# Attention over a cached context for one token: values accumulated as 64 columns x 8 positions, and a reordered end

## The chip, the cores and the metric

The kernel runs on one core of a Trainium2 chip. Its engines work side by side, each on its own queue of instructions: TensorE (PE in the profile, with its weight loads as PEld), VectorE (DVE), ScalarE (ACT), GpSimd (POOL) and SyncE (SP, which here only issues DMAs). Sixteen DMA engines move data from HBM into SBUF. The metric is the device time in microseconds of one execution.

## The reference

The inputs are one token `x` of 640 values, a condition `c` of 640, caches of keys and values for 32 heads with 8192 positions of 192 values each, and weights. All numbers are 32-bit floats.

```python
mod = (_silu(c) @ w_mod).reshape(c.shape[0], 6, 1, -1)
sa, ca, ga, sb, cb, gb = (mod[:, 0], mod[:, 1], mod[:, 2], mod[:, 3], mod[:, 4], mod[:, 5])
h = _layernorm(x, axis=-1) * (1 + ca) + sa
x = x + ga * _A_ref(h, A_k_cache, A_v_cache, A_wq, A_wo)
h = _layernorm(x, axis=-1) * (1 + cb) + sb
x = x + gb * _B_ref(h, B_w1, B_b1, B_w2, B_b2)
```

`_A_ref` makes a query per head (`h @ wq`), scores all 8192 keys, takes a softmax, sums the values with its weights and multiplies the 32 x 192 results by `wo`. `_B_ref` is a two-layer network: `relu(h @ w1 + b1)` squared, times `w2`, plus `b2`; its hidden size is 1536. Keys and values are 201 MB each, the bulk of what is read.

## The kernel before

The program is fully unrolled and its order on every engine is the order in which it is written; the framework only adds the waits.

**Storage.** Everything large goes through one pool of three slots (`slot`, tag "slot") of 128 partitions, some 57 KB each. The loads are all issued by SP, in one queue, in this order: modulation weights with the first query weights (`wm0_t`), keys 0, values 0, keys 1, values 1, and so on; each takes the slot that was used three loads earlier, so that a value load waits for the keys of the head before to be worked off, and a key load for the values of the head before. A key load of the heads between also carries 1920 columns of weights (a pair's `wq` or `wo`). After keys 31 comes the first part of `wm1_t` (the last `wo` and one modulation block), after values 31 its second part (two modulation blocks), then `w1_t`, then `gw_t`: the sixth modulation block (the gate) and the twelve blocks of `w2`, in the three pieces of `W2_CUT`.

**A head.** Each partition holds 64 consecutive positions. `keys` (L177) works in four chunks of 16 positions: VectorE multiplies by the query (L184), GpSimd folds six positions in half (L187), VectorE sums nine positions (L188) and the six halves (L189), ScalarE sums one (L192). Between chunks, `between` puts in small work: `project` of the pair before (after chunk 1 of an even head), `attend` (after chunk 2 of an even head), the next `query` (after chunk 2 of an odd head); `inverse` of the head before comes after chunk 0. `softmax` (L206) takes the maximum across partitions through TensorE, and ScalarE's exponential (L216) writes each of the 64 weights 16 times, because a multiplication on a 32-column strip of TensorE wants 32 stationary columns: here two positions, 16 copies each.

**Values.** `values` (L220) makes 32 multiplications of 384 columns per head, two positions of 192 values each. The four column strips g = j % 4 take turns, and each strip accumulates its eight multiplications in 32 partitions of one PSUM bank. Rows 0 to 15 of a strip hold the sums for the first position's weights, rows 16 to 31 those for the second's; in the first half of the columns only the first are wanted, in the second half only the second. `project` (L232) picks them: two VectorE operations per head (L238, L239) with `ri`, the inverse of the softmax's sum times a two-column mask (L204). Three multiplications per pair (L242) by ones then sum over the partitions and turn the 384 results of the pair into columns; `attend` copies these (L246) and multiplies by `wo` into `att` (L250).

**The end.** After values 31: `project` and `attend` of the last pair, the residual `x1` (L297), the layernorm (L94), with the multiplications of modulation blocks 3 and 4 (`mod(3, 2, ...)`, L130) inside `scale_b`, that is, after the layernorm's second total; transposition, the first layer (L311), bias, square (L314 to L316), transposition, the gate's modulation (`mod(5, 1, ...)`), the second layer (L327) block by block, `y` (L330) and the output.

```python
        for j in range(n):
            g = j % G
            nc.tensor.matmul(ps_t[h][32 * g:32 * (g + 1), :PW], p[:, 2 * j:2 * j + 2].rearrange("p e r -> p (e r)"),
                             t[:, PW * j:PW * (j + 1)], start=(j < G), stop=(j >= n - G))
```

Of the kernel before, what the change touches and what calls it, by code (L numbers as in the profile page):

```python
# [22 lines left out]
KB = DG // 32  # L23
FB = FG // 32
PW = 2 * DH
NPAIR = H // 2
NPOS = SK // P
I = 16
# [5 lines left out]
WQ = KB * PW  # L34
HD = NPOS * DH
SLOT = HD + WO
W2_CUT = ((0, 6), (6, 5), (11, 1))
EPS = 1e-5


@with_exitstack
def block_kernel(ctx: ExitStack, tc: tile.TileContext, xc, k0, kx, k31, vc, wm0, wm1, w1, gw2, bb, out):
# [7 lines left out]
    def slot(name):  # L50
        return strm.tile([P, SLOT], F32, tag="slot", name=name, bufs=3)
# [4 lines left out]
    ones = const.tile([P, P], F32, name="ones")  # L56
    nc.vector.memset(ones, 1.0)

    mask = const.tile([P, 2], F32, name="mask")
    nc.vector.memset(mask[:, 0:1], 0.0)  # L60
    nc.vector.memset(mask[:, 1:2], 1.0)
    for g in range(G):
        nc.vector.memset(mask[32 * g:32 * g + 16, 0:1], 1.0)
        nc.vector.memset(mask[32 * g:32 * g + 16, 1:2], 0.0)
    eps_t = const.tile([P, 1], F32, name="eps_t")
    nc.vector.memset(eps_t, EPS)

# [26 lines left out]
    def layernorm(x, copies, scale1, shift, name):  # L94
# [26 lines left out]

    mods = const.tile([P, 6, DG], F32, name="mods")

    def mod(first, n, w):

        ps = psum.tile([P, 512], F32, tag="q", name=f"ps_mod{first}", bufs=2)
        for b in range(KB):
            wb = w[:, b].rearrange("p (m n) -> p m n", m=n)
            for g in range(G):
                nc.tensor.matmul(ps[32 * g:32 * (g + 1), :n * DG], e[:, b:b + 1].to_broadcast([P, 32]),  # L130
                                 wb[:, :, DG * g:DG * (g + 1)], start=(b == 0), stop=(b == KB - 1))
# [7 lines left out]
    def load(src, to, h, what):  # L139
        to[h] = slot(f"{what}{h}")  # L140
        n, w = CUTS.get((what, h), 1), src.shape[1]
        for c in range(n):
            a, b = c * HD // n, (c + 1) * HD // n if c + 1 < n else w
            nc.sync.dma_start(to[h][:, a:b], src[:, a:b])
# [3 lines left out]
        load(k0 if h == 0 else k31 if h == H - 1 else kx[h - 1], k_t, h, "k")  # L148

    def load_v(h):  # L150
        load(vc[h].rearrange("(p i) d -> p (i d)", p=P), v_t, h, "v")

    load_k(0)
    mod(0, 2, wm0_t[:, :KB * 2 * D].rearrange("p (b n) -> p b n", b=KB))
# [43 lines left out]
    ri_t, ps_t, sum_t = {}, {}, {}  # L198

    def inverse(h):  # L200
        r = work.tile([P, 1], F32, tag="r", name=f"r{h}")
        nc.vector.reciprocal(r, sum_t.pop(h))
        ri_t[h] = work.tile([P, 2], F32, tag="ri", name=f"ri{h}", bufs=3)
        nc.vector.tensor_scalar(ri_t[h], mask, r, None, op0=ALU.mult)  # L204

    def softmax(h, sc):  # L206
        mp = work.tile([P, 1], F32, tag="mp", name=f"mp{h}")
        nc.vector.tensor_reduce(mp, sc, axis=AX.X, op=ALU.max)  # L208
        ps = psum.tile([P, 512], F32, tag="sm", name=f"ps_mx{h}", bufs=2)
        nc.tensor.matmul(ps[:, :P], mp.to_broadcast([P, P]), ident, start=True, stop=True)  # L210
        nm = work.tile([P, 1], F32, tag="nm", name=f"nm{h}")
        nc.vector.tensor_reduce(nm, ps[:, :P], axis=AX.X, op=ALU.max, negate=True)  # L212

        p = work.tile([P, NPOS, 16], F32, tag="p", name=f"p{h}", bufs=1)
        sp = work.tile([P, 1], F32, tag="sp", name=f"sp{h}")
        nc.scalar.activation(p, sc[:, :, None].to_broadcast([P, NPOS, 16]), AF.Exp, bias=nm, accum_out=sp)  # L216
        sum_t[h] = total(sp, f"sum{h}")
        return p

    def values(h, p):  # L220

        t = v_t.pop(h)
        ps_t[h] = psum.tile([P, 512], F32, tag="o", name=f"ps_o{h}", bufs=3)
        n = NPOS // 2
        for j in range(n):
            g = j % G
            nc.tensor.matmul(ps_t[h][32 * g:32 * (g + 1), :PW], p[:, 2 * j:2 * j + 2].rearrange("p e r -> p (e r)"),  # L227
                             t[:, PW * j:PW * (j + 1)], start=(j < G), stop=(j >= n - G))

    os_t = {}  # L230

    def project(i):  # L232

        os_ = work.tile([P, PW], F32, tag="os", name=f"os{i}")
        for a in range(2):
            h = 2 * i + a
            o, ps, ri = os_[:, DH * a:DH * (a + 1)], ps_t.pop(h), ri_t.pop(h)
            nc.vector.tensor_scalar(o, ps[:, :DH], ri[:, 0:1], None, op0=ALU.mult)  # L238
            nc.vector.scalar_tensor_tensor(o, ps[:, DH:PW], ri[:, 1:2], o, op0=ALU.mult, op1=ALU.add)  # L239
# [16 lines left out]
    for h in range(H):  # L256
        i = h // 2
        if h:
            load_k(h)
        if h == H - 1:  # L260
            wm1_t = slot("wm1_t")
            nc.sync.dma_start(wm1_t[:, :WO + KB * D], wm1[:, :WO + KB * D])
# [12 lines left out]
        p = softmax(h, sc)  # L275
        if h == H - 1:
            mod(2, 1, wm1_t[:, WO:WO + KB * D].rearrange("p (b n) -> p b n", b=KB))
# [5 lines left out]
    nc.sync.dma_start(w1_t[:, :KB * FF], w1)  # L283
    gw_t = slot("gw_t")
    a = 0
    for b0, n in W2_CUT:
        b = KB * D + (b0 + n) * D
        nc.sync.dma_start(gw_t[:, a:b], gw2[:, a:b])
        a = b
    w1_t = w1_t[:, :KB * FF].rearrange("p (b n) -> p b n", b=KB)  # L290
    w2_t = gw_t[:, KB * D:(KB + FB) * D].rearrange("p (b n) -> p b n", b=FB)
# [25 lines left out]
    fT = columns(f, FG, "fT", work, tag="os")  # L317
# [59 lines left out]
```

## Time and profile before

| | |
|---|---|
| median of three runs | 1059.56 us (1059.51 to 1061.22) |
| profiled execution, its time | 1059.44 us |
| profiled execution, its span | 1057.7 us |
| TensorE, matmuls | 39% busy |
| VectorE | 78% |
| ScalarE | 10% |
| GpSimd | 17% |
| read from HBM | 451.82 MB, 427 GB/s over the span |
| granted TensorE clock, mean | 0.65 |

The profile is that of one execution. Its page gives the busy time of each engine, the span in 40 slices, the DMA queues, the chain of work that ended last, and the costliest groups of instructions: line, engine, operation, output<-input, shapes, count, then busy time, mean nanoseconds of one, and the idle time before them with what ended it. A landing is counted from the issue of the DMA to the arrival of its semaphore. The granted clock is a share of full speed. A multiplication of 32-bit floats stands in the trace as two matmuls and two weight loads.

### The profile page before, as it was taken

How to read it: one execution, taken by the hardware profiler on the slowest of the kernel's cores; microseconds unless marked ns; L12 is line 12 of the kernel's file. 1: busy time of each engine (PE TensorE's matmuls, PEld its weight loads, DVE VectorE, ACT ScalarE, POOL GpSimd, SP SyncE). 2: the span in 40 equal slices, each digit the busy share in tenths (PEclk: the TensorE clock that was granted, in tenths of full speed). 3: DMA queues.
4: the chain of work that ended last, by engine and by line, in shares of the span. 5: the costliest groups of instructions: out<-in, count | busy, mean ns of one | idle time of the engine just before them, and what ended most of it. 6: DMA issues, size and time to landing. Idle time of an engine off the chain costs nothing.

```text
span 1057.7 us, 7915 instructions
## 1 busy us (share of the span) xinstructions
PE 415.7 (39%) x3120; PEld 187.8 (18%) x3120; DVE 821.5 (78%) x646; ACT 110.1 (10%) x343; POOL 180.4 (17%) x134
## 2 busy tenths in 40 slices
PE   2143532435343344533344353233533334453436
PEld 1011211112121111211112121111211111121223
DVE  1976878978787986878888787897868798789962
ACT  1010011000111010110101001100011101011110
POOL 0211112211121211211212111221111221112110
PEclk9666565666656666665666666566665666666668
DMA  9999999999999999999999999999999999999997
GB/s 400 444 430 423 439 428 428 444 427 428 436 426 429 441 426 434 427 436 426 434 438 419 440 426 445 426 436 421 438 424 439 433 432 430 423 435 430 418 431 318
DMA packets 11565, 452.33 MB, mean 428 GB/s; under 512 B 1540, under 2 KB 1544, under 8 KB 1672
## 3 DMA queue, kind: packets, MB, share of 16 engines
q1 hardware_dynamic: 11240, 451.81, 99.2%
q8 instruction: 24, 0.39, 0.1%
q14 instruction: 13, 0.11, 0.0%
q10 hardware_dynamic: 288, 0.01, 0.0%
HBM read 451.82 MB, written 0.00 MB: 427 GB/s over the span
## 4 chain that ended last, share of the span: by engine, by line
DMA 43%; DVE 40%; PE 14%; ACT 2%; issue 1%; DVEq 0%; SPq 0%; ACTq 0%
DMA k<-in_kx 40%; DVE k L184 21%; DVE sc L188 13%; PE ps_o L227 10%; DVE sc L189 4%; DMA gw_t<-in_gw 2%; ACT p L216 2%; PE ps_mx L210 1%; DMA xct<-in_xc 1%; PE ps_sum L91 1%; PE ps_mod L130 1%; PE ps_q L170 1%; DVE nm L212 0%; DVE mp L208 0%; DVE ri L204 0%
## 5 line engine op out<-in xcount | busy, mean ns | idle before, releaser
L184 DVE TENSOR_TENSOR k<-k,qb 128x3072 f32<-128x3072 f32 x128 | 429.0, 3352 | 145.7 <-DMA k<-in_kx 145.7
L187 POOL TENSOR_TENSOR k<-k 128x576 f32<-128x576 f32 x128 | 179.7, 1404 | 836.0 <-DVE k L184 799.3
L188 DVE TENSOR_REDUCE sc<-k 128x9 f32<-128x1728 f32 x128 | 250.2, 1954 | 4.4
L227 PE MATMUL ps_o<-v,p 128*32 128x384 f32 x2048 | 239.3, 637 | 0.0
L210 PE MATMUL ps_mx<-ident,mp 128*128 128x128 f32 x64 | 25.4, 501 | 338.6 <-DVE mp L208 338.6
L192 ACT ACTIVATE jk<-k 128x192 f32<-128x192 f32 x128 | 46.5, 363 | 768.1 <-DVE k L184 750.0
L227 PEld LDWEIGHTS ps_o<-v,p 128*32 128x32 f32 x2048 | 75.7, 140 | 142.2 <-issue 141.6
L189 DVE TENSOR_REDUCE sc<-k 128x6 f32<-128x576 f32 x128 | 95.1, 743 | 0.1
L242 PE MATMUL ps_oT<-ones,os 128*128 128x32 f32 x96 | 26.3, 398 | 143.1 <-DVE os L239 141.1
L210 PEld LDWEIGHTS ps_mx<-ident,mp 128*128 128x128 f32 x64 | 16.0, 311 | 357.5 <-DVE mp L208 332.2
L250 PE MATMUL att<-k,oT 128*32 128x160 f32 x360 | 27.4, 474 | 75.2 <-DVE oT L246 75.2
L170 PE MATMUL ps_q<-k,hR 128*128 128x384 f32 x150 | 52.4, 497 | 0.0
L242 PEld LDWEIGHTS ps_oT<-ones,os 128*128 128x128 f32 x96 | 22.1, 308 | 156.2 <-DVE os L239 155.6
L216 ACT ACTIVATE p<-sc,nm 128x1024 f32<-128x1024 f32 x32 | 36.7, 1147 | 114.2 <-DVE nm L212 114.2
L91 PE MATMUL ps_sum<-sp,ones 128*128 128x1 f32 x64 | 18.8, 363 | 56.2 <-ACT p L216 56.2
L170 PEld LDWEIGHTS ps_q<-k,hR 128*128 128x128 f32 x150 | 27.3, 190 | 25.2 <-issue 9.4
L212 DVE TENSOR_REDUCE nm<-ps_mx 128x1 f32<-128x128 f32 x32 | 9.3, 291 | 28.5 <-PE ps_mx L210 28.5
L250 PEld LDWEIGHTS att<-k,oT 128*32 128x32 f32 x360 | 14.8, 165 | 81.4 <-DVE oT L246 77.2
L91 PEld LDWEIGHTS ps_sum<-sp,ones 128*128 128x128 f32 x64 | 16.1, 313 | 65.6 <-ACT p L216 65.6
L192 ACT ACTIVATION_READ_ACCUMULATOR jk<-k 128x1 f32 x128 | 23.9, 187 | 0.0
L130 PE MATMUL ps_mod<-wm_t,silu 128*32 128x320 f32 (+1 forms) x120 | 12.8, 608 | 14.7 <-DVE silu L120 14.7
L238 DVE TENSOR_SCALAR os<-ps_o,ri 128x192 f32<-128x192 f32 x32 | 13.1, 408 | 3.9 <-PE ps_o L227 3.9
(74 smaller groups left out, 104.4 us busy)
## 6 DMA issues: line engine op xcount, KB each, us to landing
k<-in_kx SPq DMA_DIRECT2D x29, 7104.0 KB, 26.8
v<-in_vc SPq DMA_DIRECT2D x31, 6144.0 KB, 20.7
k<-in_k SPq DMA_DIRECT2D x1, 6144.0 KB, 27.0
k<-in_k SPq DMA_DIRECT2D x4, 1536.0 KB, 19.6
v<-in_vc SPq DMA_DIRECT2D x4, 1536.0 KB, 14.8
wm_t<-in_wm SPq DMA_DIRECT2D x1, 4160.0 KB, 12.9
k<-in_kx SPq DMA_DIRECT2D x1, 4032.0 KB
w_t<-in_w SPq DMA_DIRECT2D x1, 3840.0 KB, 21.9
```

Source lines behind the costliest of these rows:

```text
L91: nc.tensor.matmul(ps[:, :1], ones, src, start=True, stop=True)
L170: nc.tensor.matmul(ps[:, :PW], hR[:, b], w[:, b], start=(b == 0), stop=(b == KB - 1))
L184: nc.vector.tensor_mul(pr, pr, q[:, None, :].to_broadcast([P, I, DH]))
L187: nc.gpsimd.tensor_add(half, half, pr[:, m:n, DH // 2:])
L188: nc.vector.tensor_reduce(sc[:, c * I:c * I + m], pr[:, :m], axis=AX.X, op=ALU.add)
L189: nc.vector.tensor_reduce(sc[:, c * I + m:c * I + n], half, axis=AX.X, op=ALU.add)
L192: nc.scalar.activation(jk, pr[:, i], AF.Copy, accum_out=sc[:, c * I + i:c * I + i + 1])
L210: nc.tensor.matmul(ps[:, :P], mp.to_broadcast([P, P]), ident, start=True, stop=True)
L216: nc.scalar.activation(p, sc[:, :, None].to_broadcast([P, NPOS, 16]), AF.Exp, bias=nm, accum_out=sp)
L227: nc.tensor.matmul(ps_t[h][32 * g:32 * (g + 1), :PW], p[:, 2 * j:2 * j + 2].rearrange("p e r -> p (e r)"), t[:, PW * j:PW * (j + 1)], star ...
L242: nc.tensor.matmul(os_t[i][:, 32 * j:32 * (j + 1)], os_[:, P * j:P * (j + 1)], ones[:, :32], start=True, stop=True)
L250: nc.tensor.matmul(att[32 * g:32 * (g + 1), :DG], oT[:, 32 * j:32 * (j + 1)], w[:, j, DG * g:DG * (g + 1)], start=(i == 0 and j == 0), sto ...
```

## The change

**Values.** The host lays the value cache out anew: each partition's 64 positions are cut into 8 groups of 8 positions, each group into 3 blocks of 64 of the 192 columns, and a block holds, column by column, its 8 positions. A head now takes 8 x 3 = 24 multiplications of 512 columns (64 columns x 8 positions). All three of a group use the same 32 stationary columns: 8 positions, 4 copies each, so that the exponential writes 256 columns and not 1024. Strip g holds value columns 64 g to 64 g + 63, in 96 partitions.

**Picking the own columns.** Row r of a strip belongs to position r // 4. `mask` is now 128 x 8 and made from the identity. `project` multiplies PSUM by the inverse and the mask in one operation over 96 x 512, then sums over the 8 positions into 64 columns. One multiplication per pair, by a block pattern `quad`, sums over the partitions and turns the results into 96 columns. The rows of `wo` are reordered by the host to match. `inverse` is the reciprocal alone.

**The end.** The gate's modulation weights move from the front of the `w2` slot to the back of the `w1` slot and have a DMA of their own; `w2` is loaded in four pieces of 6, 3, 2 and 1 blocks. The modulation of blocks 3 and 4 is cut in steps of 2, 2 and 1 of its 5 row blocks: the first before `x1`, the second after the layernorm's first total, the third where the whole was. Behind the gate's modulation stand 16 multiplications of 512 columns by ones (`WARM`), whose result nothing reads.

```diff
-W2_CUT = ((0, 6), (6, 5), (11, 1))
+W2_CUT = ((0, 6), (6, 3), (9, 2), (11, 1))
+WARM = 4
...
+    mask = const.tile([P, E], F32, name="mask")
+    nc.vector.tensor_reduce(mask, ident.rearrange("p (g e c) -> p e g c", g=G, e=E), axis=AX.XY, op=ALU.add)
+    quad = const.tile([P, 32 * NV], F32, name="quad")
+    nc.vector.memset(quad, 0.0)
+    for g in range(NV):
+        nc.vector.memset(quad[32 * g:32 * (g + 1), 32 * g:32 * (g + 1)], 1.0)
...
-        nc.vector.tensor_scalar(m, total(s, name + "_tm"), 1.0 / (copies * D), None, op0=ALU.mult)
+        tm = total(s, name + "_tm")
+        between()
+        nc.vector.tensor_scalar(m, tm, 1.0 / (copies * D), None, op0=ALU.mult)
...
-    def mod(first, n, w):
+    def mod(first, n, w, steps=(KB,)):
...
+        b = 0
+        for k in steps:
+            for b in range(b, b + k):
+                wb = w[:, b].rearrange("p (m n) -> p m n", m=n)
+                for g in range(G):
+                    nc.tensor.matmul(ps[32 * g:32 * (g + 1), :n * DG], e[:, b:b + 1].to_broadcast([P, 32]),
+                                     wb[:, :, DG * g:DG * (g + 1)], start=(b == 0), stop=(b == KB - 1))
+            b += 1
+            if b < KB:
+                yield
         nc.vector.tensor_copy(mods[:, first:first + n], ps[:, :n * DG].rearrange("p (m n) -> p m n", m=n))
+        yield
...
-        r = work.tile([P, 1], F32, tag="r", name=f"r{h}")
-        nc.vector.reciprocal(r, sum_t.pop(h))
-        ri_t[h] = work.tile([P, 2], F32, tag="ri", name=f"ri{h}", bufs=3)
-        nc.vector.tensor_scalar(ri_t[h], mask, r, None, op0=ALU.mult)
+        ri_t[h] = work.tile([P, 1], F32, tag="ri", name=f"ri{h}", bufs=3)
+        nc.vector.reciprocal(ri_t[h], sum_t.pop(h))
...
-        nc.scalar.activation(p, sc[:, :, None].to_broadcast([P, NPOS, 16]), AF.Exp, bias=nm, accum_out=sp)
+        nc.scalar.activation(p, sc[:, :, None].to_broadcast([P, NPOS, 32 // E]), AF.Exp, bias=nm, accum_out=sp)
...
-        t = v_t.pop(h)
+        t = v_t.pop(h)[:, :HD].rearrange("p (j g n) -> p j g n", g=NV, n=E * ED)
...
-        n = NPOS // 2
+        n = NPOS // E
         for j in range(n):
-            g = j % G
-            nc.tensor.matmul(ps_t[h][32 * g:32 * (g + 1), :PW], p[:, 2 * j:2 * j + 2].rearrange("p e r -> p (e r)"),
-                             t[:, PW * j:PW * (j + 1)], start=(j < G), stop=(j >= n - G))
+            for g in range(NV):
+                nc.tensor.matmul(ps_t[h][32 * g:32 * (g + 1)], p[:, E * j:E * (j + 1)].rearrange("p e r -> p (e r)"),
+                                 t[:, j, g], start=(j == 0), stop=(j == n - 1))
...
-            o, ps, ri = os_[:, DH * a:DH * (a + 1)], ps_t.pop(h), ri_t.pop(h)
-            nc.vector.tensor_scalar(o, ps[:, :DH], ri[:, 0:1], None, op0=ALU.mult)
-            nc.vector.scalar_tensor_tensor(o, ps[:, DH:PW], ri[:, 1:2], o, op0=ALU.mult, op1=ALU.add)
+            om = work.tile([P, ED, E], F32, tag="om", name=f"om{h}", bufs=1)
+            nc.vector.scalar_tensor_tensor(om[:n], ps_t.pop(h)[:n].rearrange("p (d e) -> p d e", e=E), ri_t.pop(h)[:n],
+                                           mask[:n, None, :].to_broadcast([n, ED, E]), op0=ALU.mult, op1=ALU.mult)
+            nc.vector.tensor_reduce(os_[:n, a], om[:n], axis=AX.X, op=ALU.add)
...
-        for j in range(3):
-            nc.tensor.matmul(os_t[i][:, 32 * j:32 * (j + 1)], os_[:, P * j:P * (j + 1)], ones[:, :32], start=True, stop=True)
+        nc.tensor.matmul(os_t[i][:, :n], os_[:n].rearrange("p a d -> p (a d)"), quad[:n], start=True, stop=True)
...
+    nc.sync.dma_start(w1_t[:, KB * FF:KB * (FF + D)], gb)
+    w2_t = slot("w2_t")
     for b0, n in W2_CUT:
...
+        nc.sync.dma_start(w2_t[:, b0 * D:(b0 + n) * D], w2[:, b0 * D:(b0 + n) * D])
...
+    mod_b = mod(3, 2, wm1_t[:, WO + KB * D:WO + KB * 3 * D].rearrange("p (b n) -> p b n", b=KB), (2, 2, 1))
+    next(mod_b)
     x1 = const.tile([P, DG], F32, name="x1")
...
-        mod(3, 2, wm1_t[:, WO + KB * D:WO + KB * 3 * D].rearrange("p (b n) -> p b n", b=KB))
+        next(mod_b)
...
-    hT2 = columns(layernorm(x1, 32, scale_b, lambda: mods[:, 3], "ln2"), DG, "hT2")
+    hT2 = columns(layernorm(x1, 32, scale_b, lambda: mods[:, 3], "ln2", lambda: next(mod_b)), DG, "hT2")
...
-    mod(5, 1, gw_t[:, :KB * D].rearrange("p (b n) -> p b n", b=KB))
+    next(mod(5, 1, gb_t))
+    idle = psum.tile([P, 512], F32, tag="sm", name="ps_warm", bufs=2)
+    for k in range(WARM):
+        for g in range(G):
+            nc.tensor.matmul(idle[32 * g:32 * (g + 1)], ones[:, :32], w1_t[:, k, :512], start=True, stop=True)
...
-    wo = a(A_wo).reshape(NPAIR, 3, P, D).transpose(0, 2, 1, 3).reshape(NPAIR, P, WO)
+    wo = a(A_wo).reshape(NPAIR, 2, NV, ED, D).transpose(0, 1, 3, 2, 4).reshape(NPAIR, P, WO)
...
-        "vc": np.ascontiguousarray(a(A_v_cache).reshape(H, SK, DH)),
+        "vc": a(A_v_cache).reshape(H, P, NPOS // E, E, NV, ED).transpose(0, 1, 2, 4, 5, 3).reshape(H, P, HD),
```

Here `E` = 8, `ED` = 64, `NV` = 3 and `KB` = 5.

More of the change, by code (lines that the diff above doesn't have):

```diff
@@ L25 @@
 PW = 2 * DH
+E = 8
+ED = 64
+NV = DH // ED
 NPAIR = H // 2
@@ L36, with block_kernel @@
 SLOT = HD + WO
-W2_CUT = ((0, 6), (6, 5), (11, 1))
+W2_CUT = ((0, 6), (6, 3), (9, 2), (11, 1))
+WARM = 4
 EPS = 1e-5
 @with_exitstack
-def block_kernel(ctx: ExitStack, tc: tile.TileContext, xc, k0, kx, k31, vc, wm0, wm1, w1, gw2, bb, out):
+def block_kernel(ctx: ExitStack, tc: tile.TileContext, xc, k0, kx, k31, vc, wm0, wm1, w1, gb, w2, bb, out):
     nc = tc.nc
@@ L57, in block_kernel @@
     nc.vector.memset(ones, 1.0)
[L59 to L64, printed above, removed]
+    mask = const.tile([P, E], F32, name="mask")
[4 more added lines that the diff above has]
+        nc.vector.memset(quad[32 * g:32 * (g + 1), 32 * g:32 * (g + 1)], 1.0)
     eps_t = const.tile([P, 1], F32, name="eps_t")
@@ L92, in total, with layernorm @@
         return ps[:, :1]
-    def layernorm(x, copies, scale1, shift, name):
+    def layernorm(x, copies, scale1, shift, name, between=lambda: None):
         n = x.shape[1]
@@ L122, in block_kernel @@
     mods = const.tile([P, 6, DG], F32, name="mods")
-    def mod(first, n, w):
+    def mod(first, n, w, steps=(KB,)):
         ps = psum.tile([P, 512], F32, tag="q", name=f"ps_mod{first}", bufs=2)
[L127 to L131, printed above, removed]
+        b = 0
[8 more added lines that the diff above has]
+                yield
         nc.vector.tensor_copy(mods[:, first:first + n], ps[:, :n * DG].rearrange("p (m n) -> p m n", m=n))
+        yield
     wm0_t = slot("wm0_t")
@@ L150, in load_v @@
     def load_v(h):
-        load(vc[h].rearrange("(p i) d -> p (i d)", p=P), v_t, h, "v")
+        load(vc[h], v_t, h, "v")
     load_k(0)
-    mod(0, 2, wm0_t[:, :KB * 2 * D].rearrange("p (b n) -> p b n", b=KB))
+    next(mod(0, 2, wm0_t[:, :KB * 2 * D].rearrange("p (b n) -> p b n", b=KB)))
     ma = columns(mods[:, 0:2].rearrange("p m n -> p (m n)"), 2 * DG, "ma")
@@ L212, in softmax @@
         nc.vector.tensor_reduce(nm, ps[:, :P], axis=AX.X, op=ALU.max, negate=True)
-        p = work.tile([P, NPOS, 16], F32, tag="p", name=f"p{h}", bufs=1)
+        p = work.tile([P, NPOS, 32 // E], F32, tag="p", name=f"p{h}", bufs=1)
         sp = work.tile([P, 1], F32, tag="sp", name=f"sp{h}")
-        nc.scalar.activation(p, sc[:, :, None].to_broadcast([P, NPOS, 16]), AF.Exp, bias=nm, accum_out=sp)
+        nc.scalar.activation(p, sc[:, :, None].to_broadcast([P, NPOS, 32 // E]), AF.Exp, bias=nm, accum_out=sp)
         sum_t[h] = total(sp, f"sum{h}")
@@ L276, in block_kernel @@
         if h == H - 1:
-            mod(2, 1, wm1_t[:, WO:WO + KB * D].rearrange("p (b n) -> p b n", b=KB))
+            next(mod(2, 1, wm1_t[:, WO:WO + KB * D].rearrange("p (b n) -> p b n", b=KB)))
         values(h, p)
@@ L283, in block_kernel @@
     nc.sync.dma_start(w1_t[:, :KB * FF], w1)
-    gw_t = slot("gw_t")
-    a = 0
+    nc.sync.dma_start(w1_t[:, KB * FF:KB * (FF + D)], gb)
+    w2_t = slot("w2_t")
     for b0, n in W2_CUT:
-        b = KB * D + (b0 + n) * D
-        nc.sync.dma_start(gw_t[:, a:b], gw2[:, a:b])
-        a = b
+        nc.sync.dma_start(w2_t[:, b0 * D:(b0 + n) * D], w2[:, b0 * D:(b0 + n) * D])
+    gb_t = w1_t[:, KB * FF:KB * (FF + D)].rearrange("p (b n) -> p b n", b=KB)
     w1_t = w1_t[:, :KB * FF].rearrange("p (b n) -> p b n", b=KB)
-    w2_t = gw_t[:, KB * D:(KB + FB) * D].rearrange("p (b n) -> p b n", b=FB)
+    w2_t = w2_t[:, :FB * D].rearrange("p (b n) -> p b n", b=FB)
     inverse(H - 1)
@@ L316, in block_kernel @@
     nc.vector.tensor_mul(f, f, f)
-    fT = columns(f, FG, "fT", work, tag="os")
-    mod(5, 1, gw_t[:, :KB * D].rearrange("p (b n) -> p b n", b=KB))
+    fT = columns(f, FG, "fT", work, tag="om", bufs=1)
+    next(mod(5, 1, gb_t))
[3 more added lines that the diff above has]
+            nc.tensor.matmul(idle[32 * g:32 * (g + 1)], ones[:, :32], w1_t[:, k, :512], start=True, stop=True)
     gb2 = const.tile([P, DG], F32, name="gb2")
@@ L366 @@
         "w1": rows(B_w1, KB),
-        "gw2": np.concatenate([rows(wm[:, 5 * D:], KB), rows(B_w2, FB)], axis=1),
+        "gb": rows(wm[:, 5 * D:], KB),
+        "w2": rows(B_w2, FB),
         "bb": np.concatenate([column(B_b1, FB), column(B_b2, KB)], axis=1),
```

3 lines of the change are left out of this document (2 added, 1 removed).

## The prediction

> **What bounds the kernel now.** I read the page first: engine shares and DMA queues.
>
> ```profile
> span 1057.7 us, 7915 instructions
> ...
> PE 415.7 (39%) x3120; PEld 187.8 (18%) x3120; DVE 821.5 (78%) x646; ACT 110.1 (10%) x343; POOL 180.4 (17%) x134
> ...
> q1 hardware_dynamic: 11240, 451.81, 99.2%
> ...
> q8 instruction: 24, 0.39, 0.1%
> ```
>
> No engine is full (VectorE 78%), but the loads keep all 16 DMA engines busy for 99.2% of the span, 1049.2 us of 1057.7. Nothing in the change removes a byte. What is left is 8.5 us: the start, the end, and small gaps. So the kernel is a DMA stream, and a change elsewhere matters only if it lets the stream run dry or alters what follows the last byte.
>
> Next, the waits of SP's own queue, since SP issues every load in order and sleeps until a slot is free; then the times of its issues, when loads landed, and the chain of waits.
>
> ```profile
> SPq L144 <- DVE sc L189: 605.4, 30, 24.0
> ...
> SPq L144 <- PE ps_o L227: 325.4, 31, 11.5
> ...
> 992.82 0.33 SPq L262 DMA_DIRECT2D wm_t<-in_wm  x1
> ...
> 118.36 0.33 SPq L144 DMA_DIRECT2D v<-in_vc  x1
> ...
> 129.69 0.33 SPq L144 DMA_DIRECT2D k<-in_kx  x1
> ...
> 1003.84 2.49 SPq L144 DMA_DIRECT2D v<-in_vc  x4
> ...
> v<-in_vc SPq DMA_DIRECT2D x1, 6144.0 KB, 19.8
> ...
> wm_t<-in_wm SPq DMA_DIRECT2D x1, 2560.0 KB, 15.6
> ...
> 123.68 3.37 DVE k L184
> ```
>
> A value load is released by the keys of the head before (VectorE, L189), a key load by the values of the head before it (TensorE, L227). How much stream lies ahead at each issue is the margin. At 118.36, after the keys of an even head, key load 3 is under way and lands at 123.68: 5.3 us (after an odd head it is more, as projections run in even heads). At 129.69, after values 2, that value load is still to come, to 118.36 + 19.8 = 138.2: 8.5 us. At 1003.84, the last value load, the load before lands at 992.82 + 15.6 = 1008.4: 4.6 us. These three margins decide whether the body stays hidden.
>
> How long before the queue is short does an issue have to come? Two stretches bound it, the very start and one of the 5.3 us issues (at 873.37, key load landing at 878.70); the last columns are granted clock, DMA share and GB/s.
>
> ```profile
> 0.73 13.03 DMA xct<-in_xc
> ...
> 1.75:2.00 0.25, 0.00 (x0) 0.00 (x0) 0.00 (x0) 0.25 (x1) 0.00 (x0) 1.00 5.62 1464
> ...
> 873.37 0.33 SPq L144 DMA_DIRECT2D v<-in_vc  x1
> ...
> 875.00:876.00 1.00, 0.00 (x0) 0.00 (x0) 0.00 (x0) 1.00 (x2) 0.00 (x0) 0.50 0.63 269
> ...
> 877.00:878.00 1.00, 1.00 (x12) 0.28 (x8) 0.00 (x0) 0.00 (x0) 0.00 (x0) 0.50 0.84 344
> ...
> 878.70 3.37 DVE k L184
> ```
>
> The first loads are issued at 0.73, and their bytes move in the quarter from 1.75: within 1.3 us. At 873 the share falls to 0.63 and 0.84 up to 4.6 us after it. So some of the 16 engines, those ahead of the slowest, already run dry here; the slowest sets the landing and had just enough.
>
> **The end** is the last 35 us of the chain, with issues, landings, timeline rows of weight loads (a row is a round of four matmuls: its own time and the idle time before it) and a stretch's clock.
>
> ```profile
> 1018.25 0.33 SPq L283 DMA_DIRECT2D w_t<-in_w  x1
> ...
> 1029.88 1.28 SPq L288 DMA_DIRECT2D gw_t<-in_gw  x3
> ...
> 1024.48 5.38 PE ps_o L227 x64
> ...
> 1030.25 22.08 DMA gw_t<-in_gw
> ...
> 1052.38 1.88 PE ps_y L327 x48
> ...
> 1054.28 0.34 DVE y L330
> ...
> w_t<-in_w SPq DMA_DIRECT2D x1, 3840.0 KB, 21.9
> ...
> gw_t<-in_gw SPq DMA_DIRECT2D x1, 3520.0 KB, 18.6
> ...
> gw_t<-in_gw SPq DMA_DIRECT2D x1, 320.0 KB, 22.4
> ...
> 998.02 0.20 PEld L227 LDWEIGHTS ps_o<-v,p 128*32 128x32 f32 x4 [0.44 <-issue]
> ...
> 1025.45 0.12 PEld L227 LDWEIGHTS ps_o<-v,p 128*32 128x32 f32 x4 [0.20 <-issue]
> ...
> 1035.90 5.56 PE L130 MATMUL ps_mod<-wm_t,silu 128*32 128x320 f32 x40
> ...
> 1043.51 3.43 PE L311 MATMUL ps_f<-w_t,hT 128*32 128x384 f32 x40 [2.05 <-DVE hT L77]
> ...
> 1036.00:1037.00 1.00, 1.00 (x12) 0.33 (x16) 0.16 (x1) 0.26 (x1) 0.00 (x0) 0.50 1.08 453
> ```
>
> w1 lands at 1018.25 + 21.9 = 1040.2. Of the three pieces issued from 1029.88 on, gate and w2 blocks 0 to 5 land at 1029.88 + 18.6 = 1048.5 and blocks 6 to 10 at 1030.25 + 22.08 = 1052.3; TensorE then has six blocks left, 48 matmuls, 1.88 us, though block 11 (320 KB, issued at some 1030.7) is there at 1053.1. y starts at 1054.28, and the span ends 3.4 us later.
>
> **The change, part by part.** Times are against this execution's own 1059.44 (span 1057.7 and 1.74 around it), 0.12 below the median 1059.56.
>
> The operations that the trace lacks are scaled from these groups:
>
> ```profile
> L239 DVE SCALAR_TENSOR_TENSOR os<-ps_o,ri,os 128x192 f32<-128x192 f32 x32 | 13.4, 418 | 1.1
> ...
> L238 DVE TENSOR_SCALAR os<-ps_o,ri 128x192 f32<-128x192 f32 x32 | 13.1, 408 | 3.9 <-PE ps_o L227 3.9
> ...
> L204 DVE TENSOR_SCALAR ri<-mask,r 128x2 f32<-128x2 f32 x32 | 7.3, 229 | 1.1
> ...
> L189 DVE TENSOR_REDUCE sc<-k 128x6 f32<-128x576 f32 x128 | 95.1, 743 | 0.1
> ...
> L216 ACT ACTIVATE p<-sc,nm 128x1024 f32<-128x1024 f32 x32 | 36.7, 1147 | 114.2 <-DVE nm L212 114.2
> ...
> L227 PE MATMUL ps_o<-v,p 128*32 128x384 f32 x2048 | 239.3, 637 | 0.0
> ```
>
> *Values.* A pass of 384 columns takes a round of four column groups 0.20 + 0.44 = 0.64 us early in a burst (998.02) and 0.12 + 0.20 = 0.32 once the clock is full (1025.45). Before, 32 multiplications in two passes make 16 rounds; after, 24 in three groups make 16 rounds too, of 512 columns: 0.85 and 0.43 us. The mean burst is 239.3/32 = 7.5 us, about 7.4 slow rounds (4.7 us) and 8.6 fast. After, 4.7 us hold 5.5 slow rounds and 10.5 fast ones take 4.5: 9.2 us, **+1.7** per head. Bounds: +0 if 512 columns go as well as four groups, +6 if all rounds stay slow (16 x 0.85 = 13.6).
>
> *Exp.* 256 columns instead of 1024. From 1147 ns here, at most in proportion to 287, I take 0.43 us: **-0.7** ahead of values, bounds -0.9 and 0.
>
> *Project and inverse.* Per head two operations of 408 and 418 ns on 192 columns go. In come a masked multiply of 512 and a sum of 512 to 64. The 576-column sum takes 743 ns, so 512 about 0.68; the multiply 0.75 (the rate of that row, 1.29 ns a column, gives 0.66 at the least fixed cost, 418 ns scaled by 512/192 gives 1.11 at most). That is +0.6 a head, two heads on each even head's keys; the 229 ns of L204 go from every head. Keys of an even head get **+1.0** longer (bounds 0.6 to 1.7), odd ones 0.2 shorter. VectorE's idle wait for key loads covers its own time; the value load behind the keys comes later instead. Three transposing multiplications become one; wo's rows are reordered to match, at no cost.
>
> *What that does to the three margins.* After an even head's keys: 5.3 - 1.0 = 4.3 us. Key load after even values: 8.5 - (1.0 - 0.7 + 1.7) = 6.5. Last value load: 4.6 - 1.9 = 2.7. The 6.5 lies above every time at which a short queue was seen (4.6): free. The 2.7 lies between 1.3 and 4.6: cost 0 to 1.9, taken **+0.2**, since at the start an empty queue was served in 1.3. The 4.3 occurs 15 times: 0 if the slowest engine is served within 4.3, at most 0.97 x 15 = 14.6 if it is not; I take **+0.5** for a few short gaps, because the low shares at 873 came from engines ahead of the slowest.
>
> The Trainium skill, "DMA: Bandwidth & Descriptors", section "Latency and other measured facts", puts the first byte of this kind of DMA at about 600 ns. By it neither margin costs anything and the sum below would be 0.7 us lower; the start here, where the quarter from 1.75 is the first with bytes, puts it above that.
>
> *Start.* The mask now waits for the identity of GpSimd and quad is set; VectorE otherwise waits at this place for the 13.03 us of the first small load, so nothing is added.
>
> *Fewer instructions.* TensorE's values lose 32 of 128 (matmuls and loads) per head, 1024 in all; with the transposes (-128), L204 (-32) and the new filler (+64) some 1120 of 7915 go, 14%, or 3.4 of the 24 instruction packets. One is 0.39 MB/24 = 16 KB, 0.6 us of one DMA engine. The slowest may be spared none or one: **-0.3** (0 to -0.6).
>
> *The end.* Keys 31 end as before. Exp -0.7, the multiplications of L130 start earlier, values 31 last 16 rounds of 0.43 once the clock is full: they end 1.6 later, near 1031.4. The last projection takes 1.46 instead of 0.9, attend ends 2.0 later, 1034.9. Then the 5.56 us of L130 (at clock 0.50) are cut into 2, 2 and 1 blocks beside the layernorm's VectorE work. At full clock 2 blocks take 1.1 us, and only the third and the copy stay on the chain: hT2 is ready at 1040.8 instead of 1043.5 (1043.3 at 0.50: 2 blocks, then 2.2 us, stand on TensorE ahead of the layernorm's second total, 1.1 longer than VectorE's work there). w1 lands at 1040.2 in the stream's order, so 3.43 us of L311 end at 1044.3, f is transposed at 1046.5, gb (now behind w1) is there at 1044 and its multiplications end by 1045.9. The warming multiplications, 8 rounds of 0.43, end at 1049.3: they delay the first six w2 blocks (landed 1048.5) by 0.8, to 1051.2. Blocks 6 to 8 land at 1050.8, 9 and 10 at 1052.3, the last at 1053.1 (0.77 us a block, from 48.5 to 52.3 for five). Only 8 matmuls, 0.35 us with their start, follow 1053.1; y then starts at 1053.5 instead of 1054.28: **-0.75**. Two more DMAs on SP's queue cost about 0.7 us of issue there, 12 us ahead of need: nothing.
>
> Sum: -0.75 - 0.3 + 0.2 + 0.5 = -0.35, so 1059.1 against 1059.44, or 1059.2 beside the median.
>
> **The rivals.**
> *The queue runs dry in the body* (slower). Place: the issue of the value load after each even head's keys. For it: the 0.63 and 0.84 shares. Against it: the key load at 878.70 landed on schedule. It decides once the queue needs more than 4.3 us for the slowest engine. Price up to 14.6, half of that more likely: 1063 to 1074.
> *Three column groups do not overlap fully* (slower). Each round would last longer. For it: nothing in the rows shows three groups. Against it: four groups take 0.64 us a round early in a burst, and a single 128-wide pass of 384 columns (L170) takes 0.34 + 0.30 = 0.64 as well, so groups overlap whole. A round a quarter longer, 16 x 0.11 = 1.8 us at full clock, puts values 31 and the last value load that much later; chain and stream lose up to 1.9: 1061.1.
>
> ```profile
> 25.35 0.34 PEld L170 LDWEIGHTS ps_q<-wm_t,hR 128*128 128x128 f32 x1 [0.30 <-issue]
> ```
>
> The Trainium skill, "TensorE: Matmul & The Clock Gate", Part 3, lists a gain of 2.38 for three column tiles of 512, which would be about that quarter; the rows of four groups in the time of one speak against it.
> *The filler holds up w2* (slower). If the clock falls to 0.50 at 1035 as it did before, hT2 comes at 1043.3; then 3.4 of L311, 1.6 of gb and 3.4 of filler reach 1051.7, and twelve blocks of 0.31 follow: 1055.4 instead of 1052.38 + 1.88, so +1.1 where the forecast has -0.75: 1061.0.
> *More gain* (faster): no gaps and a whole packet spared give 1059.44 - 0.75 - 0.6 = 1058.1. More would need the 8.5 us outside the transfers to shrink further, and behind 1053.1 only 0.7 can go.
>
> **How the numbers follow.** What a measurement here can tell from no change is 0.2%, 2.1 us. Forecast, 1058.1 to 1060.3: 0.67. Dry queue 0.13, all slower. Three groups 0.07, half slower. Filler 0.08, a quarter slower. A still better end, below 1057.4: 0.05. Faster 0.05, same 0.77, slower 0.18. The range from 1057.8 to 1062.8 takes in the middle three and leaves out most of the dry queue.
>
> **What would show it.** Values bursts near 9.2 us; VectorE groups of about 0.75 and 0.68 us in project; the even heads' value issue 4.3 us ahead of the key landing; DMA share of q1 unchanged at 99%; clock at 1.00 from 1025 to the end; the last multiplications 0.3 us after the last landing. Wrong would be: dips in the slices, later key landings by the same step in each pair, or ps_y waiting for the filler rather than a DMA.

## The result

The changed kernel takes 1065.18 us (median of ten runs, 1061.21 to 1069.19) against 1059.69 for the kernel before (1059.30 to 1061.22): a ratio of 1.0049, 95% interval 1.0037 to 1.0061. It is slower by more than the 0.2% that a measurement here can tell, and its runs scatter over 8 us where those of before scatter over 2. The forecast was 1059.2, no change, in a range up to 1062.8. The profiled execution took 1063.31, one of the shorter ones, with a span of 1061.5 against 1057.7.

The page of the changed kernel: engine shares and DMA queues.

```profile
span 1061.5 us, 6822 instructions
...
PE 457.5 (43%) x2576; PEld 168.2 (16%) x2576; DVE 834.8 (79%) x609; ACT 89.6 (8%) x343; POOL 180.3 (17%) x134
...
q1 hardware_dynamic: 11528, 451.81, 99.1%
...
q8 instruction: 20, 0.33, 0.1%
```

The same bytes move, and the engines still are 99% busy. The share of idle time accounts for 1.1 us of the 3.8 by which the span grew (0.9% of 1061.5 against 0.8% of 1057.7, each rounded to within 0.5 us); the rest is counted as busy, so the share alone doesn't show where the loss lies. The groups that are new, as busy time and mean ns:

```profile
L237 PE MATMUL ps_o<-v,p 128*32 128x512 f32 x1536 | 290.6, 731 | 0.0
...
L249 DVE SCALAR_TENSOR_TENSOR om<-ps_o,ri,mask 96x512 f32<-96x512 f32 x32 | 23.7, 741 | 7.0 <-PE ps_o L237 5.4
...
L226 ACT ACTIVATE p<-sc,nm 128x256 f32<-128x256 f32 x32 | 16.2, 507 | 114.2 <-DVE nm L222 114.2
...
L251 DVE TENSOR_REDUCE os<-om 96x64 f32<-96x512 f32 x32 | 21.8, 682 | 1.1
```

Every new operation has about the price that was forecast: values 290.6/32 = 9.1 us a head (9.2), the masked multiply 0.74 (0.75), the sum 0.68 (0.68), the exponential 0.51 (0.43). So the loss is no operation's price.

Where it lies shows in the chain of waits by its steps "keys of a head begin, as their load has landed", here for heads 3 and 29, and in the issue of the value load just before each. Before:

```profile
936.03 0.33 SPq L144 DMA_DIRECT2D v<-in_vc  x1
...
941.42 3.37 DVE k L184
```

After:

```profile
122.93 3.37 DVE k L196
...
944.12 3.37 DVE k L196
...
118.72 0.33 SPq L156 DMA_DIRECT2D v<-in_vc  x1
...
939.35 0.33 SPq L156 DMA_DIRECT2D v<-in_vc  x1
```

From head 3 to head 29 the kernel before takes 941.42 - 123.68 = 817.74 us, the changed one 821.19. That is +3.45 in the stretch that the stream of loads should bound. Before it 0.75 is gained (122.93 against 123.68), behind it 1.1 lost. The loss is spread: from one odd head's key landing to the next, 9 of these 13 steps take 62.64 or 62.65 us before, and 4 are longer; after, only 3 are that short (62.66 or 62.67), and 10 are longer, by up to 1.3 us. At head 3 the value load is issued 4.2 us ahead of the key landing, as forecast (4.3), and 4.2 is the median of all 14 such loads (5.3 before). At head 29 it is 4.8, yet the landing is late: the stretch from issue to landing itself, as one window, with DMA share and GB/s in the last two columns, before and after:

```profile
936.03:941.42 5.39, 3.44 (x20) 1.80 (x24) 0.47 (x3) 1.24 (x2) 0.00 (x0) 0.50 1.06 440
```

```profile
939.35:944.12 4.77, 3.46 (x13) 1.58 (x16) 0.47 (x2) 0.60 (x2) 0.00 (x0) 0.50 0.95 351
```

Before, the 16 engines move 440 GB/s through this stretch; after, 351, with a share of 0.95. Single stretches differ by up to 100 GB/s, and this one is among the slowest of the 14; on average they have some 430 before and 400 after. The stream slows between the issue and the landing.

The end, in the chain, with the two issues, the landing of the last piece of w2 and the step into it:

```profile
1021.53 0.33 SPq L294 DMA_DIRECT2D w_t<-in_w  x1
...
1034.33 1.75 SPq L298 DMA_DIRECT2D w_t<-in_w  x4
...
w_t<-in_w SPq DMA_DIRECT2D x1, 320.0 KB, 21.1
...
1027.12 7.18 PE ps_o L237 x48
...
1037.68 1.89 PE ps_mod L138 x16
...
1040.10 1.77 PE ps_mod L138 x16
...
1042.18 0.72 PE ps_mod L138 x8
...
1044.95 4.93 PE ps_f L323 x40
...
1049.89 1.36 PE ps_mod L138 x40
...
1051.25 3.43 PE ps_warm L335 x32
...
1054.68 3.30 PE ps_y L343 x96
...
1058.01 0.34 DVE y L346
```

The chain has no DMA in it any more: from values 31 on, TensorE is the bound. From the end of keys 31 (when w1 is issued) to y it takes 1058.01 - 1021.53 = 36.5 us; before, 1054.28 - 1018.25 = 36.0. The last piece, issued near 1035.7 as the fourth of the group, is there at 1056.8; the second layer runs from the filler's end to 1057.98 without a pause and waits for none of its pieces.

### The profile page after: what moved, and what is told of

It reads as the page before. It is cut to its first block, busy times and chain, and to the rows that moved or that the text cites. A ratio compares the mean times of both kernels' runs of the same rounds, so it can differ in the third digit from the quotient of the medians.

```text
span 1061.5 us, 6822 instructions
## 1 busy us (share of the span) xinstructions
PE 457.5 (43%) x2576; PEld 168.2 (16%) x2576; DVE 834.8 (79%) x609; ACT 89.6 (8%) x343; POOL 180.3 (17%) x134
## 3 DMA queue, kind: packets, MB, share of 16 engines
q1 hardware_dynamic: 11528, 451.81, 99.1%
## 4 chain that ended last, share of the span: by engine, by line
DMA 40%; DVE 40%; PE 18%; ACT 1%; issue 1%; DVEq 0%; ACTq 0%
DMA k<-in_kx 39%; DVE k L196 21%; PE ps_o L237 13%; DVE sc L200 13%; DVE sc L201 4%; PE ps_mod L138 1%; PE ps_mx L220 1%; DMA xct<-in_xc 1%; ACT p L226 1%; PE ps_sum L95 1%; PE ps_q L182 1%; PE ps_f L323 0%; DVE nm L222 0%; DVE mp L218 0%; PE ps_warm L335 0%
## 5 line engine op out<-in xcount | busy, mean ns | idle before, releaser
L237 PE MATMUL ps_o<-v,p 128*32 128x512 f32 x1536 | 290.6, 731 | 0.0
L237 PEld LDWEIGHTS ps_o<-v,p 128*32 128x32 f32 x1536 | 68.6, 131 | 193.7 <-issue 193.0
L253 PE MATMUL ps_oT<-quad,os 96*128 96x96 f32 x32 | 11.6, 465 | 161.6 <-DVE os L251 161.6
L253 PEld LDWEIGHTS ps_oT<-quad,os 96*128 96x128 f32 x32 | 7.8, 303 | 176.1 <-DVE os L251 176.1
L249 DVE SCALAR_TENSOR_TENSOR om<-ps_o,ri,mask 96x512 f32<-96x512 f32 x32 | 23.7, 741 | 7.0 <-PE ps_o L237 5.4
L226 ACT ACTIVATE p<-sc,nm 128x256 f32<-128x256 f32 x32 | 16.2, 507 | 114.2 <-DVE nm L222 114.2
L251 DVE TENSOR_REDUCE os<-om 96x64 f32<-96x512 f32 x32 | 21.8, 682 | 1.1
```

What stands on the lines that cost most here:

```text
L237: nc.tensor.matmul(ps_t[h][32 * g:32 * (g + 1)], p[:, E * j:E * (j + 1)].rearrange("p e r -> p (e r)"), t[:, j, g], start=(j == 0), stop=( ...
L249: nc.vector.scalar_tensor_tensor(om[:n], ps_t.pop(h)[:n].rearrange("p (d e) -> p d e", e=E), ri_t.pop(h)[:n], mask[:n, None, :].to_broadca ...
```

## The experiments

Theory A, formed from these views: the value load after an even head's keys is issued too late for the DMA queue, since project grew by 1 us there; the loss is the sum of short gaps. Theory B: the new end costs. Theory C: the longer bursts of values delay the key loads. Ratios are to the kernel before in the same session, with 95% intervals.

**One half alone: the values.** The new values, exponential, projection and layouts; the end as before. The first line is against the kernel before, the others against the changed one.

```diff
+        t = v_t.pop(h)[:, :HD].rearrange("p (j g n) -> p j g n", g=NV, n=E * ED)
...
-W2_CUT = ((0, 6), (6, 3), (9, 2), (11, 1))
-WARM = 4
+W2_CUT = ((0, 6), (6, 5), (11, 1))
```

> The new values, exponential and projection with the old end. Theory A, the value loads after even heads come too late (their margin fell from 5.3 to about 4.3 us in the trace): nearly the whole loss is here, 1063 to 1066 us, with runs scattered over several us. Theory B, the new end is what costs: within 1 us of before, about 1060 us, and runs close together.

Measured: 1068.4 us (1064.95 to 1072.72), ratio 1.0083 [1.0064, 1.0101]. Theory A's part is here, and 2 us beyond its range. In its profiled execution (1072.72, the longest) the end is 2.3 us longer than in the changed kernel, from w1's issue to y:

```profile
1028.78 0.33 SPq L285 DMA_DIRECT2D w_t<-in_w  x1
...
1034.38 8.21 PE ps_o L228 x48
...
1067.53 0.34 DVE y L332
```

That is 38.75 us against 36.5 in the changed kernel and 36.0 before. Of the 2.3 us against the changed kernel, 1.0 lies in the last burst of values (8.21 us here, 7.18 there), which both kernels have alike; the other 1.2 is what the new end takes back, in one execution of each. The rest of the 3 us between the two medians, whose runs scatter by 8, isn't accounted for.

**The other half: the end.** The changed kernel with the old values, exponential and projection.

```diff
-        t = v_t.pop(h)[:, :HD].rearrange("p (j g n) -> p j g n", g=NV, n=E * ED)
+        t = v_t.pop(h)
```

> The old values with the new end (pieces of w2, steps of the modulation, filler). Theory A: no loss, 1058.5 to 1060 us, runs close together. Theory B: 1063 us or more.

Measured: 1059.83 us (1058.92 to 1062.0), ratio 1.0001 [0.9992, 1.0010]. Theory B falls. But the 0.75 us that the prediction gave to the end is not there either. The chain of this execution, and the first layer (L321) as a window, whose third number from the right is the mean clock:

```profile
1018.21 22.19 DMA w_t<-in_w
...
1040.54 5.56 PE ps_f L321 x40
...
1046.10 1.36 PE ps_mod L135 x40
...
1047.45 3.43 PE ps_warm L333 x32
...
1050.89 3.30 PE ps_y L341 x96
...
1054.21 0.34 DVE y L344
...
1040.54:1046.10 5.56, 5.56 (x48) 2.13 (x52) 0.00 (x0) 0.00 (x0) 0.00 (x0) 0.61 1.00 425
```

The first layer takes 5.56 us here and not 3.43, at a mean clock of 0.61; with the filler behind it, y starts at 1054.21 against 1054.28 in the kernel before.

**Moving VectorE's work out of the even heads.** The changed kernel, but each head's masked multiply and sum are done in the next head's keys: the pair's first in the odd head, the second in the even one. No operation goes.

```diff
             if c == 1 and h % 2 == 0 and h:
                 project(i - 1)
+            elif c == 1 and h % 2:
+                project_half(i, 0)
```

> The changed kernel, but the first head of a pair is projected in the odd head's keys and only the second in the next even head's, so that 1.4 us of VectorE work leave the even heads; nothing else differs. Theory A: the margin of the value loads after even heads returns to 5.5 us or more, the body's loss of 3 to 5 us goes, 1059.5 to 1061 us, scatter below 2 us. If instead the longer values bursts delay the key loads, nothing changes: 1064 to 1066 us.

Measured: 1059.88 us (1059.01 to 1061.66), ratio 1.0004 [0.9996, 1.0013]. The whole loss is gone, with the bursts of values as long as in the changed kernel. The value load behind head 2, the key landing that follows it, and the stretch from the issue of value load 29 to the key landing in this kernel:

```profile
117.81 0.33 SPq L156 DMA_DIRECT2D v<-in_vc  x1
...
123.59 3.37 DVE k L196
...
934.26:941.07 6.81, 5.50 (x19) 1.95 (x22) 0.47 (x2) 0.60 (x2) 0.00 (x0) 0.50 1.05 454
```

The margin is 5.8 us at head 3, which is the median of the 14, and 6.8 at head 29; the rate is 454 GB/s there, some 430 on average. Theory C isn't excluded by this alone, since the key loads behind even values are issued earlier too, 8.7 us ahead and not 7.2 as in the changed kernel.

**A delay alone, in the kernel before.** Two sums on VectorE, whose results are not used, after the projection in even heads.

```diff
                 project(i - 1)
+                if h < H - 2:
+                    delay()
```

> The kernel before, with two idle sums of some 1.05 us together added on VectorE after the projection in even heads 2 to 28; the results are not used. The value load behind these keys comes that much later: margin 5.3 down to about 4.2 us, as in the changed kernel, with nothing else of it. If the late value load is the cause: 1063 to 1067 us with a scatter of several us. If the longer values bursts or the heavier TensorE are needed for the loss: 1059.5 to 1060.5 us.

Measured: 1064.79 us (1062.58 to 1068.04), ratio 1.0049 [1.0035, 1.0063]. This is the loss of the change, scatter included, with none of its values and nothing of its end. The median margin is 4.3 us, and the key loads behind even values keep 8.7 (8.9 before), so the loss needs no longer bursts of values, and theory C falls as its cause. The sums' group, and the same stretch:

```profile
L170 DVE TENSOR_REDUCE idle_t<-hR 128x1 f32<-128x640 f32 x14 | 11.3, 809 | 0.0
...
L171 DVE TENSOR_REDUCE idle_t<-hR 128x1 f32<-128x256 f32 x14 | 5.7, 409 | 0.0
...
942.91:947.26 4.35, 2.40 (x12) 1.40 (x16) 0.48 (x3) 1.24 (x2) 0.00 (x0) 0.50 0.95 400
```

**The same delay in odd heads.**

```diff
+            elif c == 1 and h % 2 == 1 and h < H - 1:
+                delay()
```

> The same two idle sums in odd heads 1 to 29 of the kernel before, where the margin of the value load is about 9 us. If the margin is what counts: no change, 1059.3 to 1060 us. If it is VectorE's load as such, the same loss as with the sums in even heads.

Measured: 1060.61 us (1059.33 to 1061.12), ratio 1.0005 [0.9997, 1.0014]. As much VectorE work, where the margin is wide: no loss that can be told. The margin there is less than the expectation said: 7.1 us before and 6.1 with the sums, by the medians of the traces. It is the margin and not the load of VectorE.

**Half and twice the delay in even heads.** One sum of 384 columns; and the two sums twice. Both cuts are against the kernel with the delay.

```diff
-        nc.vector.tensor_reduce(idle_t[:, 0:1], hR, axis=AX.XY, op=ALU.add)
-        nc.vector.tensor_reduce(idle_t[:, 1:2], hR[:, :2], axis=AX.XY, op=ALU.add)
+        nc.vector.tensor_reduce(idle_t[:, 0:1], hR[:, :3], axis=AX.XY, op=ALU.add)
```

> The kernel before with one idle sum of about 0.5 us in even heads 2 to 28: margin 4.8 us. With an edge just below 5.3 us a third to a half of the loss of the 1.16 us delay: 1061 to 1062.5 us; with an edge at 4.3 us nothing: 1059.5 to 1060 us.

```diff
                     delay()
+                    delay()
```

> The kernel before with twice the idle sums (some 2.3 us) in even heads 2 to 28: margin 5.3 down to 3.0 us. If the queue needs a fixed time of about 4.3 us for all engines, each of 14 pairs loses the whole further 1.2 us: 1077 to 1083 us. If only some engines now and then are late: 1068 to 1073 us.

Measured: half 1060.21 us (1059.34 to 1061.36), ratio 1.0002 [0.9993, 1.0011]; twice 1071.4 us (1070.32 to 1076.41), ratio 1.0116 [1.0094, 1.0138]. By median and pair of heads (14 of them): 0.5 us later costs nothing that can be told, 1.0 us costs 5.2/14 = 0.37, 2.1 us 11.8/14 = 0.84. The edge lies between a margin of 4.8 and 4.3 us, and beyond it the next microsecond costs some 0.4, not 1. The page of the double delay and the same stretch:

```profile
span 1074.6 us, 7971 instructions
...
q1 hardware_dynamic: 11240, 451.81, 98.4%
...
953.47:956.73 3.26, 1.31 (x4) 1.00 (x4) 0.47 (x2) 1.24 (x2) 0.00 (x0) 0.50 0.74 244
```

A margin of 3.3 us, and 244 GB/s. The page has 1.6% of the span idle, 17.2 us against 8.5 before: about half of the 16.9 us that this execution is longer. The other half is counted as transfers that take longer; why isn't shown.

All kernels together, with the median margin of the 14 value loads behind even heads 2 to 28, the mean rate from their issue to the key landing, and the ratio to the kernel before (margins and rates are from one execution each):

| | margin, us | GB/s | ratio |
|---|---|---|---|
| split projection | 5.8 | 430 | 1.0004 |
| before | 5.3 | 433 | |
| delay in odd heads | 5.3 | 415 | 1.0005 |
| half the delay | 4.8 | 406 | 1.0002 |
| delay | 4.3 | 374 | 1.0049 |
| the change | 4.2 | 401 | 1.0049 |
| twice the delay | 3.2 | 281 | 1.0116 |

The ratio follows the margin. The rate does so only roughly: half the delay has about that of the change, and no loss.

**Value loads in four pieces.** In the changed kernel, and in the one with the split projection.

```diff
-        n, w = CUTS.get((what, h), 1), src.shape[1]
+        n, w = CUTS.get((what, h), 4 if what == "v" else 1), src.shape[1]
```

> The changed kernel with every value load cut into four DMAs of 1536 KB, issued one after the other. If a DMA engine waits because the description of a load of 6 MB takes its time to reach all engines, the first quarter reaches them sooner and most of the loss goes: 1060 to 1062.5 us. If the wait is a fixed time from issue to first byte: no change, 1064 to 1067 us, or a little more for the extra DMAs.

> The projection split over odd and even heads and the value loads in four pieces together. If both act on the same short queue, nothing more is to be had than with the split alone: 1059 to 1060.5 us; if the pieces cost more than they bring with the margin restored, above 1061.

Measured: 1066.86 us (1066.76 to 1070.33), ratio 1.0079 [1.0067, 1.0091]; with the split 1066.16 us (1065.84 to 1067.68), ratio 1.0067 [1.0054, 1.0080]. By their numbers the second branch of each expectation holds: no change or a little more without the split, above 1061 with it. The first of the two proves little, since the pieces cost 6.3 us where the margin is restored (1066.16 against 1059.88). With pieces the split brings 0.7 us (1066.86 to 1066.16), without them 5.3; whether the first quarter reaches the engines sooner, or the pieces' own cost hides the late issue, can't be told. The page of the split one with pieces, whose share stands against 99.2% of the split one alone:

```profile
q1 hardware_dynamic: 24920, 451.82, 99.5%
```

The same bytes go in 24920 packets instead of 11528, and the engines are not idle but busy for longer: 6.3 us for 837 more packets on each of 16 engines, 7.5 ns each if it is the packets; the 93 additional DMAs were not tried apart from them.

**The filler.** The changed kernel without its 16 multiplications, and the split one without them.

```diff
-WARM = 4
+WARM = 0
```

> The changed kernel without the 16 filler multiplications. If these hold up the second layer as the trace after shows (they end at 1054.7, after the first six blocks have landed), the end is 0.5 to 1 us shorter: 1064.3 us. If they hold the clock up for the second layer: 0 to 1 us longer. The scatter of the body stays either way.

> The changed kernel with the split projection and without the filler. If the filler keeps the clock of the second layer up at no cost: 0.5 to 2 us longer than the 1059.9 us of the split with it. If it only holds up the second layer: 0.3 to 0.8 us shorter.

Measured: 1067.04 us (1064.77 to 1070.23), ratio 1.0069 [1.0056, 1.0081]; with the split 1059.69 us (1059.29 to 1060.29), ratio 0.9999 [0.9990, 1.0008]. Without the body's scatter the filler makes no difference (1059.69 against 1059.88), so neither branch of that expectation holds. Both sides of it can be seen in the profiles, first the changed kernel without filler, then the split one without:

```profile
1056.72 5.25 PE ps_y L342 x96
```

```profile
1051.16 1.02 PE L351 MATMUL ps_y<-w_t,fT 128*32 128x160 f32 x24 [0.31 <-DMA w_t<-in_w]
...
1052.73 1.25 PE L351 MATMUL ps_y<-w_t,fT 128*32 128x160 f32 x24 [0.54 <-DMA w_t<-in_w]
```

In the one, after TensorE had stood idle for 3.2 us, 96 matmuls took 5.25 us and not 3.30, at a mean clock of 0.67 and with two waits for pieces of w2 among them. In the other TensorE had stood idle for 1.4 us, and the blocks again wait for their pieces.

**The best of both.** The old values, their projection split over odd and even heads, and the new end.

```diff
+            elif c == 1 and h % 2:
+                project_half(i, 0)
```

> The old values with the old projection split over odd and even heads (margin after even heads about 6.1 us) and the new end. If the kernel before already loses a little to the short queue: 1058 to 1059 us and less scatter. If its slowest DMA engine never waited: 1059.3 to 1060 us, as with the new end alone.

Measured: 1059.42 us (1059.03 to 1060.69), ratio 0.9997 [0.9989, 1.0006]. The kernel before lost nothing that can be told to the short queue, and nothing tried here beats it.

## Why the prediction was wrong

**The mechanism was there, as the first rival; its chance and the forecast's price were wrong.** The prediction found the three margins, said that 4.3 us would be left after even heads, and named the point from which it decides. The step that failed is the price in "What that does to the three margins": "I take +0.5 for a few short gaps, because the low shares at 873 came from engines ahead of the slowest". In its place the change lost 5.5 us, and the delay alone, at a margin of 4.3, costs 5.2: 0.37 for each of 14 loads, where +0.5 over 15 had 0.03. (Head 0 has no projection before it, so 14 loads come later and not 15.) The reason given doesn't hold. The rows beside the two low shares, from the same trace, are high:

```profile
874.00:875.00 1.00, 0.40 (x2) 0.11 (x1) 0.29 (x1) 0.17 (x1) 0.00 (x0) 0.50 1.38 545
...
876.00:877.00 1.00, 0.88 (x6) 0.70 (x10) 0.00 (x0) 0.07 (x1) 0.00 (x0) 0.50 1.05 401
```

In windows of 1 us the share swings all over the trace of the kernel before: 0.66 in 895 to 896, 11 us behind an issue, and between 0.34 and 1.79 from 862 to 948. A window's share can exceed 1, as 5.62 did at the start, so it counts more than its own time. The stretch from the issue at 873.37 to the landing has 0.98. So 0.63 and 0.84 don't show engines running dry, nor which of them is the slowest. What the prediction did have was a landing on time at a margin of 5.3, which bounds the time that is needed by 5.3 and says nothing on 4.3. The upper bound of 14.6 was safe; half of it, 7.3, which the rival called more likely, was near the 5.5 measured. Twice the delay (margin 3.2) costs 11.8. Why a load has to come that early stays open.

**The range.** It left most of the dry queue out at a chance of 0.13. No row stood behind so low a chance: the start, with 1.3 us, shows the first bytes only, and 5.3 was the smallest margin behind even heads that had been seen to cost nothing. Between bounds of 0 and 14.6 that left the price open.

**Values, projection, exponential: right.** All within 0.1 us of the forecast, and so was the margin, 4.2 us. The three column groups do overlap whole. Two rounds of three in the changed kernel, early and late in a burst:

```profile
1003.28 0.19 PEld L237 LDWEIGHTS ps_o<-v,p 128*32 128x32 f32 x3 [0.66 <-issue]
...
1004.77 0.12 PEld L237 LDWEIGHTS ps_o<-v,p 128*32 128x32 f32 x3 [0.31 <-issue]
```

They take 0.85 and 0.43 us, as worked out from whole overlap, and 16 of them 9.1 on average. That rival falls, and with it the 2.38 of the Trainium skill's "TensorE: Matmul & The Clock Gate", Part 3, for this shape.

**The first byte.** The Trainium skill's "DMA: Bandwidth & Descriptors", "Latency and other measured facts", has about 600 ns; by it the margin of 4.2 us would have cost nothing. The delay experiments contradict its use as the time that the queue needs: a margin of 4.8 us costs nothing that can be told, 4.3 costs 0.37 a load. What takes the rest of that time isn't shown. The start isn't above the 600 ns for certain, either: the issue at 0.73 takes 0.39 us itself, and from its end the first quarter with bytes lies 0.6 to 0.9 us on.

**The key load after even values (margin 6.5) free: right as far as can be told.** Such a load waits for the values of two heads earlier. Its margin is 7.2 us in the changed kernel (8.9 before). No run has that alone: the split brings it back to 8.7, but so has the delay in even heads, which loses as much as the change; and value loads behind odd heads cost nothing at 6.1. **The last value load: +0.2 is not confirmed.** Its margin is 3.7 us and not 2.7. From the landing of keys 29 to the end of keys 31 the changed kernel takes 0.6 us more than the kernel before, and the runs don't say what of it is this load's; but the split kernel has this margin at 3.1 and loses nothing that can be told.

**The end: -0.75 forecast, nothing found.** With the old values the new end gives 0.07 at y and a ratio of 1.0001. Two of its terms failed. "3.43 us of L311": it took 4.93 in the changed kernel and 5.56 in the end alone, at a mean clock of 0.69 and 0.61. And so the filler ended late, at 1054.68, 33.2 us behind keys 31 where 31.1 was forecast. That is the third rival, the filler that holds up w2, in part, and by another way than it named: in the end alone the first layer's input was ready in time, and the layer itself ran slowly. Even where the end goes as foreseen, in the split kernel, nothing is gained: the last piece lands at 1034.35 + 19.61 = 1053.96 us, not at 1053.1, and y starts at 1054.56. With the new values the new end seems to earn some 1.2 us against the old one, by one execution of each.

**Fewer instructions: -0.3 was a guess** that the runs can't confirm: the instruction packets fell from 24 to 20, about as forecast (3.4), and no time can be put to it.

## What to carry to other kernels

In a kernel bound by its loads, look for the issue that has the least stream ahead of it, and count what every edit adds between the landing that wakes an engine and that issue; an engine with 20% idle time can cost you there. A landing that was on time shows that its margin was enough, and nothing about a smaller one: price the microseconds below the smallest margin seen as open, up to the whole of them, and let the range have that. Before you read a dip in a window of 1 us, look at its neighbours and at windows far from any issue. Runs that start to scatter are a sign of a margin used up (8 us here where the kernel before has 2); small work could then be moved to the step where the margin is wide, at no cost that can be told.

## What the runs showed of the hardware

A load of 6 MB behind a running one had to be issued some 4.3 to 4.8 us ahead of the end of that one to cost nothing that can be told (5.2 us over 14 loads at 4.3), though at the start of the kernel the first bytes moved within 1.3 us. What takes this time isn't shown. Cutting the value loads into pieces of 12 KB per partition instead of 48 cost 6.3 us in all, 7.5 ns for each additional packet on an engine if it is the packets that cost.
